# Moving a token-block border of an interleaved second GEMM next to an AV run, and one filler step with it

## The chip, the cores and the metric

The kernel runs on one core of a Trainium2 chip. The metric is the device time of a run in microseconds (us), the median over the runs of one kernel. The span of a profiled execution goes from the first to the last instruction and is some 2 us shorter than the run's time. All runs used here were classed as being in the fast state. Some of them show a granted TensorE clock of 0.988 to 0.995 instead of 1.0 and are 1 to 3 us longer; where such runs matter, this is said. Others are as much longer at a clock of 0.999 to 1.0 (350.76 us for the kernel before, 347.15 for one of the variants); why is not known. Small differences between median times are therefore not relied on alone here, but with the distances within a stage, which repeat almost exactly.

## The reference

Attention with a decay ("forgetting") term for 8 batches of 8 heads, 576 tokens and head size 64, then a two-layer network with the exact GELU on the 4608 token rows:

```python
scores = scale * q @ k.T ; decay = cum[:, :, :, None] - cum[:, :, None, :]     # cum = cumsum(log(clip(f)))
attn   = softmax(where(causal, scores + decay, -1e9))
x      = (attn @ v)  -> rows of 512
h      = x @ w_in                  # 512 -> 2048
out    = gelu(h) @ w_out           # 2048 -> 512
```

## The kernel before

Batches come one after another. An attention stage works through four pairs of heads, and each pair has four score tiles (0 to 3): matmuls into a PSUM tile with two buffers, an exp on ScalarE that reads it, and a mask on GpSimd (POOL). ScalarE can't keep up with bare score matmuls (an exp of a 128x896 tile takes 0.92 us, the matmuls of that tile 0.36), so TensorE does the **second GEMM of the previous batch** between the score tiles. This filler comes in steps from a generator. After tile 1 of each pair come the 30 matmuls of attention times V (the "AV run") of the pair before.

```python
PLAN = [                                   # token block, who lends the two banks, the 16 steps
    (0, "o", 16 * "r"),
    (1, "m", 6 * "r" + "n" + 9 * "r"),
    (2, "m", "n" + 9 * "r" + "n" + 5 * "r"),
    (3, "s", 7 * "r" + 9 * "n"),
]

def gemm2_rows(c, plan):
    for ts, held, steps in plan:
        ...                                # banks[0], banks[1]: two PSUM tiles of the pool "held"
        for kt, step in enumerate(steps):
            last = kt == steps.rindex("r")
            for r in range(2 if step == "r" else 1):
                rows = slice(r * D, (r + 1) * D) if step == "r" else slice(0, P)
                nc.tensor.matmul(banks[r], g_of[c][kt][rows, ...], w_out_sb[rows, kt, :], ...)   # L466
            if kt == n_ff - 1 if held == "s" else last:
                nc.vector.tensor_copy(ot, banks[1])                                              # L474
            if kt == n_ff - 1:
                nc.vector.tensor_tensor(ot, ot, banks[0], Alu.add)                               # L476
                store(c, ts, ot)
            yield

FILL = [[7, 6, 3, 3], [1, 3, 3, 3], [1, 3, 3, 3], [1, 3, 3, 3], [7]]     # steps after tile t of pair i

def attention(b):                          # b = 2 takes other counts and another plan
    ...
    for i in range(HP):
        for t in range(4):
            scores(b, i, t)                # score matmuls L289, exp L299, mask L301
            take(fill, counts[i][t])
            if i and t == 1:
                av(i - 1)                  # AV run L320, then normalize on DVE (L333, L334)
            ...
    take(fill, counts[HP][0])
    av(HP - 1)
    take(fill, 6)
    ...
    take(fill, 999)
```

An "r" step is two matmuls of 64 rows into two banks, which use the two halves of the array side by side (both matmuls of the r step at 198.88 us lie within 0.38 us, and one alone takes 0.38), as the score matmuls do (two at 198.68 within 0.36). An "n" step is one matmul of all 128 rows into banks[0], as the AV matmuls are. At the end of a block DVE copies banks[1] out and adds banks[0] to it. Blocks 1 and 2 both take the two banks of pool "m", which has just two. The bank that the copy frees is the one that block 2 gets as banks[0]: in the trace the n step that opens block 2 starts at 202.27 us, right after the copy (201.52 to 202.21) and during the add (202.25 to 202.94). After the attention stage comes the first GEMM of the batch (L375), with GELU on ScalarE.

The softmax here doesn't subtract the row's maximum and nothing guards it: scores larger than these inputs give would overflow.

Of the kernel before, what the change touches and what calls it, by code (L numbers as in the profile page):

```python
# [52 lines left out]
def kernel(  # L53
# [340 lines left out]
    def gemm2(c):  # L394
# [35 lines left out]

    PLAN = [
        (0, "o", 16 * "r"),
        (1, "m", 6 * "r" + "n" + 9 * "r"),
        (2, "m", "n" + 9 * "r" + "n" + 5 * "r"),
        (3, "s", 7 * "r" + 9 * "n"),
    ]

# [8 lines left out]
    def gemm2_rows(c, plan):  # L446




        for ts, held, steps in plan:
            if held == "s":
                both = s_psum.tile([P, 2, d_model], FP32, tag="s", name="ps2")
                banks = [both[:, 0], both[:, 1]]
            else:
                pool = {"o": o_psum, "m": m_psum}[held]
                banks = [
                    pool.tile([P, d_model], FP32, tag=held, name="ps2")
                    for _ in range(2)
                ]  # L460
            ot = o_pool.tile([P, d_model], FP32, tag="ot", name="ot")
# [4 lines that stand above are left out]
                    nc.tensor.matmul(  # L466
                        banks[r],
                        g_of[c][kt][rows, ts * P : (ts + 1) * P],
                        w_out_sb[rows, kt, :],
                        start=kt == (steps.index("r") if r else 0),  # L470
                        stop=last if r else kt == n_ff - 1,
# [7 lines that stand above are left out]
# [37 lines left out]
    def gemm2_third():  # L516
        yield from gemm2_half(0, 1)
        yield from gemm2_rows(0, PLAN_0)
        yield from gemm2_rows(1, PLAN_1)
# [94 lines left out]



    FILL = [[7, 6, 3, 3], [1, 3, 3, 3], [1, 3, 3, 3], [1, 3, 3, 3], [7]]
    FILL_2 = [[8, 8, 8, 8], [8, 8, 4, 4], [4, 4, 4, 4], [4, 4, 4, 4], [8]]
    FILL_1 = [[0, 0, 0, 0], [0, 0, 0, 0], [2, 2, 2, 2], [2, 2, 2, 2]]

    def attention(b):


        fill = gemm2_third() if b == 2 else gemm2_rows(b - 1, PLAN)
        counts = FILL_2 if b == 2 else FILL

# [135 lines left out]
```

## Time and profile before

| | before |
|---|---|
| time, median of 3 runs (range) | 348.35 us (348.30 to 348.62) |
| span of the profiled run | 345.7 us |
| TensorE busy | 328.3 us, 95% |
| TensorE's idle time ahead of the filler, waiting for the DVE copy L474 | 3.9 us in 5 waits |
| from the start of AV run 0 in one stage to that in the next | 36.16 us |

In a line of the grouped view the figures after the first bar are the busy time in us and the mean ns of one instruction; after the second bar stands the idle time of the engine just before these instructions, and what ended most of it. In a timeline line they are the start, the duration, the engine, the line of the program, the operation and its count; what stands in brackets is the idle time before it and its releaser. Lines that follow each other on one engine are merged, so a count of six is three r steps.

### The profile page before, as it was taken

Reading aid. Unit: us, or ns where it says so; the run is one execution under the profiler, and the core shown is the slowest. Engines: PE = TensorE matmul, PEld = TensorE weight load, DVE = VectorE, ACT = ScalarE, POOL = GpSimd, SP = SyncE. Lnnn points to the kernel's source line nnn. Section 1 sums busy time; section 2 is a strip of 40 time slices with the busy share of each in tenths; the row PEclk is TensorE's granted clock in tenths of the full one; section 3 lists DMA queues with packets and bytes.
Section 4 is the critical chain, followed back from the end, with each engine's and each line's share of the span. In section 5 each row is a group of like instructions: output and inputs, shape, how many; then the busy total and the mean of one; then the engine's idle time right before and its main releaser. Section 6 shows DMA issues by size and latency. Waiting matters only on the chain.

```text
span 345.7 us, 7895 instructions
## 1 busy us (share of the span) xinstructions
PE 328.3 (95%) x3187; PEld 173.7 (50%) x3227; DVE 188.1 (54%) x424; ACT 212.1 (61%) x296; POOL 125.1 (36%) x256
## 2 busy tenths in 40 slices
PE   7899999999999999999899989998999899999995
PEld 3674555445554455545554555445544554444443
DVE  5670456934367935795479647974597542020011
ACT  5976786773634787368746874687468765503600
POOL 8390673128418044533345333624261430000000
PEclk9999999999999999999999999999999999999999
DMA  8999999979992999488935995498900230011013
GB/s 116 176 171 194 202 178 147 170 149 161 222 183 100 138 202 176 81 119 167 219 89 81 134 211 137 74 161 190 170 30 2 69 83 30 2 61 61 0 35 89
DMA packets 99924, 43.03 MB, mean 124 GB/s; under 512 B 78704, under 2 KB 95344, under 8 KB 99888
## 3 DMA queue, kind: packets, MB, share of 16 engines
q1 hardware_dynamic: 82592, 28.37, 42.4%
q0 software_dynamic: 16896, 13.63, 26.9%
q8 instruction: 25, 0.41, 0.5%
q10 hardware_dynamic: 400, 0.52, 0.4%
q14 instruction: 11, 0.09, 0.1%
HBM read 36.85 MB, written 9.44 MB: 134 GB/s over the span
## 4 chain that ended last, share of the span: by engine, by line
PE 89%; DVE 4%; ACT 3%; issue 2%; POOL 2%; POOLq 0%; ACTq 0%; DVEq 0%
PE ps L375 35%; PE ps L466 25%; PE o L320 9%; PE ps L408 8%; PE s L289 8%; ACT e L299 2%; PE ps L501 2%; PE ps_x L353 1%; DVE ot L474 1%; PE ps_f L206 1%; DVE x L334 1%; POOL q L107 1%; POOL k L107 1%; DVE qT L213 0%; DVE kT L213 0%
## 5 line engine op out<-in xcount | busy, mean ns | idle before, releaser
L392 ACT ACTIVATE g<-ps 128x512 bf16<-128x512 f32 x144 | 85.3, 597 | 80.2 <-PE ps L375 80.2
L299 ACT ACTIVATE e<-s 128x896 bf16<-128x896 f32 (+2 forms) x128 | 101.0, 836 | 32.1 <-PE s L289 28.2
L375 PE MATMUL ps<-xT,w_in_sb 128*128 128x512 bf16 x497 | 111.4, 379 | 0.8
L466 PE MATMUL ps<-w_out_sb,g 64*128 64x512 bf16 (+1 forms) x736 | 104.0, 376 | 4.7 <-DVE ot L474 3.9
L375 PEld LDWEIGHTS <-w_in_sb 128*128 128x128 bf16 x576 | 56.0, 98 | 67.5 <-issue 1.8
L301 POOL TENSOR_SCALAR_AFFINE_SELECT e<-e 128x256 bf16<-128x256 bf16 (+1 forms) x135 | 49.5, 385 | 100.1 <-ACT e L299 99.9
L466 PEld LDWEIGHTS <-g 64*128 64x128 bf16 (+1 forms) x756 | 39.8, 94 | 40.4 <-issue 10.6
L244 DVE COPY qT<-tq 64x288 bf16<-64x288 bf16 x96 | 49.3, 514 | 1.4
L260 POOL TENSOR_TENSOR vw<-v_sb,wT 128x640 bf16<-128x640 f32 x31 | 39.6, 1279 | 24.7 <-DMA v_sb<-in_v_dram 24.5
L289 PE MATMUL s<-qT,kT 64*128 64x320 bf16 (+4 forms) x384 | 43.9, 277 | 3.3 <-ACT e L299 2.6
L320 PE MATMUL o<-vw,e 128*128 128x65 bf16 x960 | 36.8, 194 | 2.7 <-issue 2.4
L320 PEld LDWEIGHTS <-e 128*128 128x128 bf16 x960 | 34.8, 98 | 9.2 <-POOL e L301 4.1
L474 DVE COPY ot<-ps 128x512 f32<-128x512 f32 x26 | 17.9, 690 | 35.5 <-PE ps L466 35.5
L244 DVE COPY kT<-tk 64x288 bf16<-64x288 bf16 x96 | 33.0, 344 | 1.6
L334 DVE TENSOR_TENSOR x<-o,r 128x320 bf16<-128x320 f32 x64 | 31.5, 492 | 2.2
L417 DVE COPY ot<-ps 128x512 f32<-128x512 f32 (+2 forms) x9 | 5.7, 632 | 48.8 <-PE ps L408 31.9
L289 PEld LDWEIGHTS <-kT 64*128 64x128 bf16 x384 | 18.7, 94 | 22.6 <-issue 7.3
L333 DVE RECIPROCAL r<-o 128x5 f32<-128x5 f32 x64 | 12.2, 190 | 30.8 <-PE o L320 30.7
L408 PE MATMUL ps<-w_out_sb,g 128*128 128x512 bf16 (+2 forms) x142 | 27.9, 355 | 0.1
L408 PEld LDWEIGHTS <-g 128*128 128x128 bf16 x144 | 13.5, 98 | 14.5
L476 DVE TENSOR_TENSOR ot<-ot,ps 128x512 f32<-128x512 f32 x26 | 17.9, 687 | 1.2
L375 PE MATMUL ps<-tails,w_in_sb 128*128 128x512 bf16 x63 | 14.3, 377 | 0.1
(64 smaller groups left out, 148.2 us busy)
## 6 DMA issues: line engine op xcount, KB each, us to landing
out_dram<-ot SPq DMA_DIRECT2D x32, 256.0 KB, 2.3
v_sb<-in_v_dram SPq DMA_DIRECT2D x24, 256.0 KB, 5.7
q<-in_q_dram POOLq DMA_DIRECT2D x6, 576.0 KB, 6.2
k<-in_k_dram POOLq DMA_DIRECT2D x6, 576.0 KB, 8.2
v_sb<-in_v_dram SPq DMA_DIRECT2D x22, 128.0 KB, 5.3
w_in_sb<-in_moe_w_in_dram POOLq DMA_DIRECT2D x4, 512.0 KB, 7.0
w_out_sb<-in_moe_w_out_dram POOLq DMA_DIRECT2D x4, 512.0 KB, 8.4
q<-in_q_dram POOLq DMA_DIRECT2D x4, 144.0 KB, 4.5
```

What stands on the lines that cost most here:

```text
L244: nc.vector.tensor_copy(rows[:, odd], src[odd * D : (odd + 1) * D, 2 * i + h].rearrange("d j p -> d p j"),)
L260: eng.tensor_tensor(vw_of[b][:, hs, :, 0:D], v_sb[:, hs, :, :], w.unsqueeze(3).to_broadcast([P, 2, NBLK, D]), Alu.mult,)
L289: nc.tensor.matmul(to, *ab, start=half < 0, stop=half == 1 or not masked)
L299: nc.scalar.activation(et[:, :, z:c], st[:, :, z:c], Act.Exp, scale=scale)
L301: nc.gpsimd.affine_select(out=et[:, :, c0 + z : c0 + P], in_=et[:, :, c0 + z : c0 + P], compare_op=Alu.is_ge, fill=0.0, base=z, pattern=[[ ...
L320: nc.tensor.matmul(o[:, m, :], e_of[b, i, t][:, h, c : c + P], vw_of[b][:, 2 * i + h, n, :], start=(n == 0), stop=(n == m),)
L334: nc.vector.tensor_tensor(x_of[b, i][:, :, h, :], o[:, :, 0:D], r.unsqueeze(2).to_broadcast([P, NBLK, D]), Alu.mult,)
L375: nc.tensor.matmul(ps, w_in_sb[:, kt, ffb * P : (ffb + 1) * P], src[:, kt, 0:TC], start=(kt == 0), stop=(kt == n_dm - 1),)
L392: nc.scalar.activation(g_of[c][ffb], ps, Act.Gelu)
L408: nc.tensor.matmul(pss[ts][:, c0:c1], g_of[c][kt][:, ts * P : (ts + 1) * P], w_out_sb[:, kt, c0:c1], start=(kt == 0), stop=(kt == n_ff - 1),)
L466: nc.tensor.matmul(banks[r], g_of[c][kt][rows, ts * P : (ts + 1) * P], w_out_sb[rows, kt, :], start=kt == (steps.index("r") if r else 0), ...
L474: nc.vector.tensor_copy(ot, banks[1])
```

## The change

The border between blocks 1 and 2 moves from one step ahead of AV run 1 to AV run 1 itself, so that the eviction of block 1 can lie beside the AV matmuls. For this the fill gives up one step after tile 3 of pair 1 and takes it back ahead of AV run 3; the n steps are placed again so that each AV run follows one.

```diff
-        (1, "m", 6 * "r" + "n" + 9 * "r"),
-        (2, "m", "n" + 9 * "r" + "n" + 5 * "r"),
+        (1, "m", 6 * "r" + "n" + 8 * "r" + "n"),
+        (2, "m", 9 * "r" + "n" + 6 * "r"),
...
-    FILL = [[7, 6, 3, 3], [1, 3, 3, 3], [1, 3, 3, 3], [1, 3, 3, 3], [7]]
+    FILL = [[7, 6, 3, 3], [1, 3, 3, 2], [1, 3, 3, 3], [1, 3, 3, 3], [8]]
```

The five stages of batches 3 to 7 use these tables.

## The prediction

> **Names.** An attention stage (batches 3 to 7, so five of them) runs four head pairs, 0 to 3, and for each pair four score tiles, 0 to 3. Between score tiles it puts filler: 64 steps of the previous batch's second GEMM, 16 for each of four token blocks. An r step is two 64-row matmuls into two PSUM banks, an n step is one 128-row matmul into one bank. AV p is the run of 30 AV matmuls of pair p, issued after tile 1 of pair p+1. Steps are numbered 0 to 63.
>
> **What bounds the kernel now.** I read the page first: engine shares, then the chain of waits.
>
> ```profile
> PE 328.3 (95%) x3187; PEld 173.7 (50%) x3227; DVE 188.1 (54%) x424; ACT 212.1 (61%) x296; POOL 125.1 (36%) x256
> PE 89%; DVE 4%; ACT 3%; issue 2%; POOL 2%; POOLq 0%; ACTq 0%; DVEq 0%
> L466 PE MATMUL ps<-w_out_sb,g 64*128 64x512 bf16 (+1 forms) x736 | 104.0, 376 | 4.7 <-DVE ot L474 3.9
> ```
>
> TensorE is the bound: 95% busy and 89% of the chain. The granted clock digit is 9 in all 40 slices, so the clock is not in question. The third line is the filler; TensorE stood idle 4.7 us before it, 3.9 of them for the DVE copy that empties a PSUM bank. The view of that copy line and the list of waits of TensorE both give this as 3.9 us in 5 waits, longest 0.8: one for each of the five stages. From 123 us on, where the five stages lie, the list has nothing else but 2.4 us of "issue" ahead of AV runs; the other waits lie in the first two batches, which the change doesn't touch. The timeline of TensorE in one stage (batch 4) shows where the wait is:
>
> ```profile
> 196.71 0.33 PE L289 MATMUL s<-qT,kT 64*128 64x64 bf16 x4
> 196.88 0.60 PE L466 MATMUL ps<-w_out_sb,g 64*128 64x512 bf16 x4
> 197.63 1.12 PE L320 MATMUL o<-vw,e 128*128 128x65 bf16 x30 [0.16 <-issue]
> ...
> 200.72 0.33 PE L289 MATMUL s<-qT,kT 64*128 64x64 bf16 x4
> 200.88 0.60 PE L466 MATMUL ps<-w_out_sb,g 64*128 64x512 bf16 x4
> 202.27 0.38 PE L466 MATMUL ps<-w_out_sb,g 128*128 128x512 bf16 x1 [0.79 <-DVE ot L474]
> 202.48 1.11 PE L320 MATMUL o<-vw,e 128*128 128x65 bf16 x30
> ```
>
> Both groups are the same work: tile 1, two r steps, an n step, an AV run. (In the first the record of the n matmul is missing, although its weight load is in the trace; hence the "issue" gap.) From tile 1 to AV 0 it takes 197.63 - 196.71 = 0.92 us, and AV 2 gives 0.92 too; to AV 1 it takes 202.48 - 200.72 = 1.76. The difference, 0.84 us, is the cost of the wait. Its reason is in the plan: step 31, an r step, ends block 1, and step 32, the n step, opens block 2 in the same two "m" banks with nothing between them.
>
> [...] the trace has 692 for the copy, 687 for the add, so the two take about 1.4 us one after the other. [...] for the two shapes of exp that matter below; the trace has 917 and 698. [...] on the chain nine r steps of batch 4 fill 0.65 us per three, 0.217 each. I use 0.21 to 0.22 us a step, r or n.
>
> **The change part by part.** It adds and removes no instruction: on every engine the program order has as many rows as before, only places differ; SyncE's order is the same.
>
> (1) Fill: tile 3 of pair 1 is followed by two steps instead of three, and the run before AV 3 gets eight instead of seven. So AV 0 still comes after step 22, AV 1 after step 31 (was 32), AV 2 after 41 (was 42), AV 3 after 55 (same).
>
> (2) Plan: block 1 ends in an n step (31), block 2 begins with an r step (32) and has its n at 41. The number of n steps and of changes between r and n is the same; each AV run still has one n step ahead of it. The border of blocks 1 and 2 now has AV 1 and tile 2 of pair 2 between its sides. The 0.79 us wait ahead of AV 1 must go: that n step now writes into its own block's open bank. **Removed: 0.84 us a stage.**
>
> (3) Does the eviction hide? Put in the clock of the stage above, before this change: the copy starts after the last r step, at 201.52, and ends at 202.21; the add runs 202.25 to 202.94. AV 1 would start at 200.72 + 0.92 = 201.64, tile 2 of pair 2 at 201.64 + 1.05 = 202.69 and step 32 some 0.20 later, at 202.89. Its first matmul goes to the bank that the copy freed long ago, the second to the one that the add frees at 202.94; with the 0.06 us that the wait in the trace took from the copy's end to the matmul (202.21 to 202.27) that is 203.00. **Left over: about 0.1 us.**
>
> (4) One step fewer between tile 3 of pair 1 and tile 0 of pair 2 brings tiles 0 and 1 of pair 2 forward by 0.21 us. There are two score buffers, so tile 1 of pair 2 needs the exp of tile 3 of pair 1 to be done. ScalarE in a stretch of that stage:
>
> ```profile
> 199.15 1.51 ACT L299 ACTIVATE e<-s 128x896 bf16<-128x896 f32 x2 [0.74 <-PE s L289]
> 199.96 0.70 ACT L299 ACTIVATE e<-s 128x640 bf16<-128x640 f32 x1
> ```
>
> The two lines are from two narrow windows; the first merges the exps of tiles 2 and 3, the second is tile 3 alone. It ends at 199.96 + 0.70 = 200.66; tile 1 started at 200.72, without a wait, only just. Tile 0 is all right: its buffer is free at 199.15 + 0.92 = 200.07, plus 0.06, and it would come at 200.10. Tile 1 would come at 200.72 - 0.21 = 200.51 and must wait until about 200.72. **New: 0.21 us**, exactly the step taken out: it becomes idle time there and is paid later, ahead of AV 3.
>
> The sum for a stage: -0.84 + 0.21 + 0.10 = -0.53 us. Five stages: -2.65 us. TensorE is on the path through the rest of the stage and the first GEMM after it, so what it gains is gained at the end: 348.35 - 2.65 = **345.7 us**, 0.8% less.
>
> **Rivals.** (A) No new wait: the removed time is all kept, 5 x 0.84 = 4.2 us, 344.15 us. For it: my figures in (3) and (4) are differences of 0.1 to 0.2 us, near the trace's grain, and the second r matmul may hide a late bank. Against: 200.72 against 200.66 is read directly, and a buffer can't be written before its exp. (B) The wait moves: the two DVE operations still take 1.4 us, and the normalize of AV 1 now queues behind both (it ends at 204.4 in the clock above, some 2.8 us after AV 1 began instead of 2.0). If the next AV run or the transpose DMA of this pair had waited for it, the gain would be gone, 348 us. Against: AV 2 comes 4.0 us after AV 1, and the transposed tile is first read at the GEMM at 213.8. (C) Another engine becomes the bound, or DMA does: ScalarE is 61% busy, and had 0.74 us idle just before the two lines above; DVE is 54%, DMA is near 9 tenths in many slices but no TensorE wait for a DMA is in the list of waits. A stage of 36.2 us that shrinks by 0.5 leaves this as it is. It would give 347 to 348.5. (D) Slower by more than the noise would need a fresh wait over 0.84 us per stage; I see none.
>
> **Range and chances.** The ground is regular: the five waits are 0.78 or 0.79 us and the three runs lie within 0.32 us. Between A (344.15) and a half-lost gain (347.2) lies most of what I can imagine; 8 in 10 for 344.5 to 347.0. Over 2% faster would be below 341.4, more than all the waits that the change can reach; over 2% slower would be 355.3. I give each 1%.
>
> **What would show it right or wrong.** In the changed trace: the wait of the filler for the copy of line 474 (3.9 us) is gone; tile 1 of pair 2 to AV 1 takes 0.92 instead of 1.76 us in each stage; a wait of tile 1 of pair 2 for an exp, some 0.2 us five times, in the list of waits; at step 32 a wait for the add of line 476 of 0.1 us or less; the stage's period falls from 36.2 to about 35.6 us; the first GEMM's stretches keep their 14 us. The prediction is wrong if tile 1 shows no such wait (then 344 to 345), if step 32 waits by several tenths, or if something later (the transposes before the first GEMM, untangling) takes back what was gained.

## The result and the profile after

| | before | changed |
|---|---|---|
| median (range), 4 runs each | 348.33 us (347.60 to 348.62) | 345.50 us (345.24 to 346.67) |
| ratio, 95% interval | 1 | 0.9928 (0.9900 to 0.9956) |
| span of the profiled run | 345.7 us | 343.4 us |

A ratio is the mean time of one kernel's fast runs over the mean of the other's fast runs of the same rounds, so it isn't quite the ratio of the medians. The change saves 0.7%, within the 2% that counts as the same.

The page of the changed kernel, engine shares and the line of the filler:

```profile
PE 328.6 (96%) x3182; PEld 174.7 (51%) x3227; DVE 187.0 (54%) x424; ACT 212.3 (62%) x296; POOL 124.2 (36%) x256
L466 PE MATMUL ps<-w_out_sb,g 64*128 64x512 bf16 (+1 forms) x731 | 103.0, 376 | 0.8 <-issue 0.8
```

The work is the same and the span is 2.3 us shorter. The 3.9 us of waits for the copy are gone.

The timeline of TensorE in the changed kernel, in the stage that the prediction showed of before, from tile 3 of pair 1 on:

```profile
198.77 0.30 PE L289 MATMUL s<-qT,kT 64*128 64x320 bf16 x2
198.91 0.59 PE L466 MATMUL ps<-w_out_sb,g 64*128 64x512 bf16 x4
199.36 0.37 PE L289 MATMUL s<-qT,kT 64*128 64x256 bf16 x4
199.55 0.39 PE L466 MATMUL ps<-w_out_sb,g 64*128 64x512 bf16 x2
199.95 0.34 PE L289 MATMUL s<-qT,kT 64*128 64x64 bf16 x4
200.12 0.61 PE L466 MATMUL ps<-w_out_sb,g 64*128 64x512 bf16 x4
200.88 1.11 PE L320 MATMUL o<-vw,e 128*128 128x65 bf16 x30 [0.16 <-issue]
201.93 0.36 PE L289 MATMUL s<-qT,kT 64*128 64x448 bf16 x2
202.13 0.97 PE L466 MATMUL ps<-w_out_sb,g 64*128 64x512 bf16 x6
202.78 0.30 PE L289 MATMUL s<-qT,kT 64*128 64x320 bf16 x1
202.91 0.38 PE L466 MATMUL ps<-w_out_sb,g 64*128 64x512 bf16 x1
202.94 0.29 PE L289 MATMUL s<-qT,kT 64*128 64x320 bf16 x1
```

Three things are to be seen. Tile 1 of pair 2 (199.95) to AV 1 (200.88) takes 0.93 us; before it took 1.76. Tile 0 to tile 1 of that pair takes 199.95 - 199.36 = 0.59 us; one r step lies between them, which makes 0.40 to 0.41 in pair 1 (195.55 to 195.96). And after AV 1 the two halves of the array fall out of step: the two matmuls of a score tile, together at 198.77 (both within 0.30 us, the time of one), start at 202.78 and 202.94.

DVE around the border, first before, then changed:

```profile
201.52 0.69 DVE L474 COPY ot<-ps 128x512 f32<-128x512 f32 x1 [1.86 <-PE ps L466]
202.25 0.69 DVE L476 TENSOR_TENSOR ot<-ot,ps 128x512 f32<-128x512 f32 x1
```

```profile
200.76 0.69 DVE L474 COPY ot<-ps 128x512 f32<-128x512 f32 x1 [1.86 <-PE ps L466]
201.56 0.69 DVE L476 TENSOR_TENSOR ot<-ot,ps 128x512 f32<-128x512 f32 x1
```

The eviction now runs from 200.76 to 202.25, beside AV 1 (200.88 on). It takes 1.49 us instead of 1.42: the add begins 0.11 us after the end of the copy (200.76 + 0.69 = 201.45) instead of 0.04.

ScalarE in the changed kernel, from two narrow windows, for the gap ahead of tile 1: the exps of tiles 2 and 3 of pair 1, and those of tile 3 and the next one:

```profile
198.39 1.51 ACT L299 ACTIVATE e<-s 128x896 bf16<-128x896 f32 x2 [0.74 <-PE s L289]
...
199.20 1.56 ACT L299 ACTIVATE e<-s 128x640 bf16<-128x640 f32 x2
```

The exp of tile 3 ends at 198.39 + 1.51 = 199.90 and tile 1 of pair 2, which takes over its buffer, starts at 199.95. In the same way the exp of tile 2 ends at 199.31 (198.39 + 0.92) and tile 0 of pair 2 starts at 199.36.

For the whole stage I measure from AV run to AV run and, at the spot above, from tile 0 to tile 1 of pair 2. The stages of one kernel agree to 0.02 us, with one exception that is named below. "Stage" is from AV 0 to the AV 0 of the next stage; columns are us.

| kernel | AV 0 to AV 1 | AV 1 to AV 2 | AV 2 to AV 3 | tile 0 to 1, pair 2 | stage |
|---|---|---|---|---|---|
| before | 4.85 | 4.00 | 4.33 | 0.41 | 36.16 |
| changed | 4.00 | 4.17 | 4.51 | 0.59 | 35.67 |

AV 0 to AV 1 has a step fewer in the changed kernel, AV 2 to AV 3 a step more. A stage gains 0.49 us, five gain 2.45. The span lost 2.3, because AV 0 of the first of these stages came 0.23 us later in the changed profile (125.53 against 125.30), where the two programs are still the same.

### The profile page after: what moved, and what is told of

Same layout as the page of the kernel before. It is cut to its first block, busy times and chain, and to the rows that moved or that the text cites. A ratio compares the mean times of both kernels' runs of the same rounds, so it can differ in the third digit from the quotient of the medians.

```text
span 343.4 us, 7895 instructions
## 1 busy us (share of the span) xinstructions
PE 328.6 (96%) x3182; PEld 174.7 (51%) x3227; DVE 187.0 (54%) x424; ACT 212.3 (62%) x296; POOL 124.2 (36%) x256
## 4 chain that ended last, share of the span: by engine, by line
PE 89%; issue 2%; POOL 2%; DVE 2%; ACT 2%; DMA 2%; POOLq 0%; ACTq 0%; DVEq 0%
PE ps L375 36%; PE ps L466 25%; PE o L320 9%; PE ps L408 8%; PE s L289 7%; PE ps L501 2%; ACT e L299 2%; DMA k<-in_k_dram 2%; PE ps_x L353 1%; DVE x L334 1%; POOL q L107 1%; PE ps_f L206 1%; POOL k L107 1%; DVE r L333 0%; DVE xT L356 0%
## 5 line engine op out<-in xcount | busy, mean ns | idle before, releaser
L466 PEld LDWEIGHTS <-g 64*128 64x128 bf16 (+1 forms) x756 | 41.5, 94 | 40.4 <-issue 11.9
L289 PE MATMUL s<-qT,kT 64*128 64x320 bf16 (+4 forms) x384 | 45.8, 276 | 3.6 <-ACT e L299 2.7
L474 DVE COPY ot<-ps 128x512 f32<-128x512 f32 x26 | 17.9, 689 | 37.1 <-PE ps L466 35.2
L289 PEld LDWEIGHTS <-kT 64*128 64x128 bf16 x384 | 19.5, 94 | 23.2 <-issue 9.7
L476 DVE TENSOR_TENSOR ot<-ot,ps 128x512 f32<-128x512 f32 x26 | 17.9, 687 | 1.5
L365 POOL COPY tails<-xT 128x256 bf16<-128x256 bf16 x8 | 3.2, 399 | 31.3 <-DVE xT L356 31.3
```

The source lines that it names most:

```text
L289: nc.tensor.matmul(to, *ab, start=half < 0, stop=half == 1 or not masked)
L466: nc.tensor.matmul(banks[r], g_of[c][kt][rows, ts * P : (ts + 1) * P], w_out_sb[rows, kt, :], start=kt == (steps.index("r") if r else 0), ...
```

## The experiments

My theory: the kernel before lost 0.84 us a stage since PSUM banks were taken again before DVE had emptied them; the changed kernel hides the eviction beside the AV run, but pays two new, smaller waits, one for an exp and one for the add. The rivals: that the order of n and r steps is what helps; that a border has to lie at an AV run, so nothing else would do; and that the two small gaps have other causes. The 95% intervals of the ratios of the changed kernel and of the versions with one remedy overlap (0.9900 to 0.9956 against 0.9879 to 0.9919 and 0.9882 to 0.9932), so what decides between them is the stage's distances in the traces. The first four kernels ran together on one chip (before: 348.23 us), the next three on another occasion (before: 348.20), the last three on a third (before: 348.11). All gave correct results.

### The plan alone

```diff
 PLAN as in the change; FILL as before
```

> The new plan (block 1 ends with an n step, block 2 opens with r) with the old fill counts, so AV 1 still comes after step 32, which is now an r step that opens block 2 ahead of AV 1. My theory (the eviction must lie beside the AV run): the opening r step now needs both banks, so it waits for copy and add, and AV 1 starts about 0.6 us later than before; two more changes between r and n add up to 0.1 us each. +0.6 to +0.9 us in each of five stages: 351.3 to 352.8 us. The rival (the plan itself, with its better order of n steps, is what helps, and the fill counts are cosmetic) expects 345 to 346 us.

Measured: 352.90 us (352.27 to 355.17), ratio 1.0141 (1.0114 to 1.0168). TensorE around the border:

```profile
167.28 0.70 PE L466 MATMUL ps<-w_out_sb,g 64*128 64x512 bf16 x3
168.45 0.37 PE L466 MATMUL ps<-w_out_sb,g 64*128 64x512 bf16 x1 [0.46 <-DVE ot L474]
169.24 0.37 PE L466 MATMUL ps<-w_out_sb,g 64*128 64x512 bf16 x1 [0.42 <-DVE ot L476]
169.54 0.42 PE L320 MATMUL o<-vw,e 128*128 128x65 bf16 x8
```

The opening r step waits twice: its first matmul for the copy, its second for the add. AV 0 to AV 1 takes 5.51 us, 0.66 more than before, and the stage 37.06, 0.90 more; 5 x 0.90 = 4.5 us, beside 4.7 in the time, just above the range expected. Of the 0.90 us, 0.22 lie between AV 1 and AV 2 (4.22 instead of 4.00), where nothing waits: n step 41 is followed by an r step ahead of AV 2, and such a lone n step has a cost that the next experiment shows. So the plan by itself is harmful: it opens the block with a step that needs both banks, and parts an n step from its AV run. Of the kernels run here, it is good only with the fill counts that bring the border to an AV run.

### The fill counts alone

```diff
 PLAN as before; FILL as in the change
```

> The old plan with the new fill counts: AV 1 comes after step 31, so the border of the blocks is at AV 1, but the n steps 32 and 42 now come after an AV run and a score tile, among r steps, and the AV runs 1 and 2 follow an r step. My theory (what counts is that the AV run lies between the last step of block 1 and the first of block 2): most of the gain stays, since the n step that opens block 2 needs only the bank freed first and then finds it free; the cost is two n steps among r steps, an estimated 0.1 to 0.2 us each a stage. About 346 to 347 us. The rival (the n step next to the AV run is the point) expects 348 us or more. Waits of 0.79 us for the copy: none.

Measured: 346.79 us (346.49 to 347.17), ratio 0.9957 (0.9942 to 0.9973). No wait for the copy or the add is in the list. Stage: 35.93 us, with 3.99 us from AV 0 to AV 1, 4.22 from AV 1 to AV 2 and 4.73 from AV 2 to AV 3. The border's place thus brings about half of the changed kernel's gain by itself (0.23 of 0.49 us a stage). What is missing against the changed kernel are its two n steps among r steps, shown by the time from tile 2 to tile 3 of pairs 2 and 3, 1.06 us each with the n step first in between (timeline of TensorE, the score matmuls alone):

```profile
166.70 0.36 PE L289 MATMUL s<-qT,kT 64*128 64x448 bf16 x2
...
167.76 0.30 PE L289 MATMUL s<-qT,kT 64*128 64x320 bf16 x2
...
170.92 0.36 PE L289 MATMUL s<-qT,kT 64*128 64x448 bf16 x2
...
171.98 0.30 PE L289 MATMUL s<-qT,kT 64*128 64x320 bf16 x2
```

With three r steps in between it is 0.84 or 0.85. A single full-array step among half-array work costs 0.21 us more than an r step. An n step among its like is no slower than an r step: six in a row take 1.30 us in the kernel before (211.76 to 213.06), 0.217 each, so I put the 0.21 us down to the two changes between whole-array and half-array work, some 0.1 us each. What in a change takes this time, no run separates. (The "up to 0.1 us each" of the plan alone and the "0.1 to 0.2 us" here were my estimates before these runs.) The sum closes: against the changed kernel 2 x 0.21 more, 0.16 less for the second small wait, which is absent here, makes +0.26 us, and the stage is 0.26 longer.

### The step taken out elsewhere

```diff
-    FILL = [[7, 6, 3, 3], [1, 3, 3, 2], ...        # changed
+    FILL = [[7, 6, 3, 3], [1, 2, 3, 3], ...
-        (1, "m", 6 * "r" + "n" + 8 * "r" + "n"),
+        (1, "m", 5 * "r" + "n" + 9 * "r" + "n"),
```

> The changed kernel, but the step is taken out after tile 1 of pair 1 (ahead of AV 0) instead of after tile 3 of pair 1; its n step moves to 21, so AV 0 still follows an n step, and the border stays at AV 1. My theory says that the changed kernel pays about 0.2 us a stage because tile 1 of pair 2 waits for the exp of tile 3 of pair 1; here the spacing of these tiles is the old one and that wait should go: tile 0 to tile 1 of pair 2 takes 0.41 us again instead of 0.59, 5 x 0.18 = 0.9 us less than the changed kernel, about 344.6 us. The rival (that gap is no wait for the exp but a delay in TensorE's own order, or the wait only moves to another tile) expects 345.5 us.

Measured: 344.59 us (344.19 to 346.11), ratio 0.9899 (0.9879 to 0.9919); again, on the third occasion, 344.84 us (344.05 to 347.21), ratio 0.9911 (0.9878 to 0.9943), beside 345.73 for the changed kernel.

> Only the step taken out ahead of AV 0, in the same rounds as the version with both: 344.6 us as before, some 0.8 us more than with both.

Tile 0 to tile 1 of pair 2 takes 0.40 us again and the stage 35.45 us, 0.22 less than in the changed kernel; 5 x 0.22 = 1.1 us. AV 0 comes one step earlier and no wait appears in its place, as ScalarE had 0.74 us idle there in the changed kernel and still has 0.53 here. The gap of 0.59 us was therefore the wait for the exp: same steps, same border, only the spacing of the tiles restored. Of the repeated runs two, at 346.7 and 347.2 us, have granted clocks of 0.995 and 0.990; the other four lie at 344.05 to 345.01. The first of the two is the profiled one. Its clock was low only ahead of the five stages (0.96 in the first 40 us, 1.00 from then on), and its stages take 35.45 us too, but for one of 35.97: there the first GEMM waited 0.35 us for the DMA that transposes x. No other profile shows this wait in the five stages.

### Two n steps at the end of block 1

```diff
-        (1, "m", 6 * "r" + "n" + 8 * "r" + "n"),       # changed
+        (1, "m", 6 * "r" + "n" + 7 * "r" + 2 * "n"),
```

> The changed kernel, but block 1 ends with two n steps instead of one (6 r, n, 7 r, 2 n), so that the copy of the second bank can start one step earlier and the add right after it. My theory: the changed kernel pays 0.16 us a stage after AV 1 since the second matmul of step 32 waits for the add; here the add ends some 0.2 us earlier and the delay goes: AV 1 to AV 2 takes 4.00 us as in the kernel before instead of 4.17, 5 x 0.16 = 0.8 us less than the changed kernel, about 344.7 us. The rival (the delay there has another cause, such as the score tiles) expects 345.5 us.

Measured: 344.59 us (344.44 to 347.15), ratio 0.9907 (0.9882 to 0.9932). TensorE, then DVE:

```profile
200.62 1.11 PE L320 MATMUL o<-vw,e 128*128 128x65 bf16 x30
201.66 0.36 PE L289 MATMUL s<-qT,kT 64*128 64x448 bf16 x2
201.86 0.81 PE L466 MATMUL ps<-w_out_sb,g 64*128 64x512 bf16 x6
202.51 0.30 PE L289 MATMUL s<-qT,kT 64*128 64x320 bf16 x2
```

```profile
200.28 0.69 DVE L474 COPY ot<-ps 128x512 f32<-128x512 f32 x1 [1.65 <-PE ps L466]
201.07 0.69 DVE L476 TENSOR_TENSOR ot<-ot,ps 128x512 f32<-128x512 f32 x1
```

The add ends at 201.76, ahead of the opening r step at 201.86; in the changed kernel it ended at 202.25, behind that step's start at 202.13. The three r steps are back to 0.81 us from 0.97, the score matmuls start as a pair, and AV 1 to AV 2 takes 4.00 us instead of 4.17. The second small wait was the one for the add. (The changed kernel was not in these rounds; its figures come from its own traces, in which AV 1 to AV 2 takes 4.16 or 4.17 us in every stage.)

### Both remedies

```diff
 FILL as with the step taken out elsewhere
+        (1, "m", 5 * "r" + "n" + 8 * "r" + 2 * "n"),
         (2, "m", 9 * "r" + "n" + 6 * "r"),
```

> Both remedies in one: the step is taken out ahead of AV 0, and block 1 ends with two n steps. If the two small losses of the changed kernel (0.18 us at tile 1 of pair 2, 0.16 us after AV 1) are what I take them for and independent, both go: 5 x 0.34 = 1.7 us less than the changed kernel, about 343.8 us. If ScalarE or the POOL masking bounds the stage at that pace, the sum will not be reached: 344.5 or more.

Measured: 344.66 us (343.62 to 347.57), ratio 0.9901 (0.9860 to 0.9942). The six runs scatter, and the profiled one of them had a granted clock of 0.988; the run doesn't decide whether the two gains add. It was repeated, with the changed kernel and the first remedy in the same rounds:

> The version with both remedies once more, since its first runs scattered (343.6 to 347.6 us) and its profiled run had a granted clock of 0.988. In the first trace its stage took 35.29 us against 36.16 before: 348.3 - 5 x 0.87 = 343.9 us. If the remedies were not additive in time, it would be no better than 344.6 us, the time of each remedy alone.

> The changed kernel in the same rounds as the two others, for a comparison on one chip: 345.6 us, 0.9 us over the step ahead of AV 0 and 1.7 us over both remedies.

Measured: 343.82 us (343.64 to 344.14, 5 runs), ratio 0.9870 (0.9843 to 0.9897); the changed kernel 345.73 us, ratio 0.9923. The difference is 1.9 us, against 1.7 expected from 5 x 0.34. The stage takes 35.29 us, in both profiles of this kernel: in the first, the low clock (0.91) lies in the first 40 us, and AV 0 of the first of the five stages comes 3.2 us later than in the second (128.70 against 125.46). Against the changed kernel that is 35.67 - 35.29 = 0.38 us a stage, so the two gains add. Of the 0.87 us gained on before, 0.84 is the old wait, which is now gone with nothing in its place:

```profile
198.72 0.36 PE L289 MATMUL s<-qT,kT 64*128 64x256 bf16 x4
198.91 0.38 PE L466 MATMUL ps<-w_out_sb,g 64*128 64x512 bf16 x2
199.13 0.33 PE L289 MATMUL s<-qT,kT 64*128 64x64 bf16 x4
199.29 0.38 PE L466 MATMUL ps<-w_out_sb,g 64*128 64x512 bf16 x2
199.83 0.38 PE L466 MATMUL ps<-w_out_sb,g 128*128 128x512 bf16 x1 [0.16 <-issue]
200.05 1.11 PE L320 MATMUL o<-vw,e 128*128 128x65 bf16 x30
```

(The 0.16 us of "issue" stands for a missing record of the first of two n steps.) Here tile 1 comes 0.41 us after tile 0 and AV 1 0.92 us after tile 1.

### The border left where it was, an earlier copy

```diff
 FILL as before
-        (1, "m", 6 * "r" + "n" + 9 * "r"),             # before
+        (1, "m", 6 * "r" + "n" + 6 * "r" + 3 * "n"),
```

> The kernel before with its old fill counts and its border ahead of AV 1, but block 1 ends with three n steps, so that its second bank is copied out three steps ahead of the border. The n step that opens block 2 then finds the bank free, and no border has to move. My theory (the cost was the 0.79 us from the last r step to the end of the copy, and nothing else about the border): the wait goes, 5 x 0.84 = 4.2 us less, less an n step among r steps (0.1 to 0.2 us a stage): 344.2 to 345.2 us. The rival (the border has to lie at an AV run) expects little: 347 to 348 us.

Measured: 345.13 us (344.73 to 345.74), ratio 0.9899 (0.9870 to 0.9927). A border need not lie at an AV run. With the last r step three steps ahead of the end, the copy runs from 163.86 to 164.55, while block 1 goes on in its other bank, and the first step of block 2 finds an empty one; the list of TensorE's waits in the five stages is empty. The loss is an n step among score tiles (the three n steps are the last before the border, and the first of them stands alone between tiles 0 and 1 of pair 2; timeline of all engines, TensorE's matmuls and DVE's copy alone):

```profile
163.66 0.35 PE L289 MATMUL s<-qT,kT 64*128 64x256 bf16 x4
...
163.86 0.69 DVE L474 COPY ot<-ps 128x512 f32<-128x512 f32 x1 [0.86 <-PE ps L466]
...
163.94 0.39 PE L466 MATMUL ps<-w_out_sb,g 128*128 128x512 bf16 x1
...
164.27 0.34 PE L289 MATMUL s<-qT,kT 64*128 64x64 bf16 x4
```

Tile 0 to tile 1 is 0.61 us here, 0.20 more than with an r step, and the stage takes 35.53 us: 0.63 less than before, as 0.84 - 0.20 gives.

### The changed kernel again

> The changed kernel once more, with the two others on one chip, so that they can be compared within the same rounds: 345.5 us.

Measured: 346.01 us (344.90 to 347.11), ratio 0.9931 (0.9898 to 0.9963). The three ratios of the changed kernel are 0.9928, 0.9931 and 0.9923. This trace also settles a point of reading: it has the records of all 756 filler matmuls, and with them the 0.16 us of "issue" ahead of the AV runs is gone, from 2.4 us to none in the list. Those gaps were missing records, not idle time. The same holds for an entry that could be taken for the new wait: the first trace of the changed kernel lists 0.8 us in 5 waits of AV runs for the add, but they are ahead of AV 3 (209.56, 0.16 us), where the n step's record is missing, and are gone from the full trace.

All kernels side by side, with the stage's distances (us):

| kernel | AV 0 to AV 1 | AV 1 to AV 2 | AV 2 to AV 3 | tile 0 to 1, pair 2 | stage |
|---|---|---|---|---|---|
| plan alone | 5.51 | 4.22 | 4.34 | 0.41 | 37.06 |
| fill alone | 3.99 | 4.22 | 4.73 | 0.59 | 35.93 |
| step out ahead of AV 0 | 4.01 | 4.16 | 4.51 | 0.40 | 35.45 |
| two n steps | 4.01 | 4.00 | 4.51 | 0.60 | 35.51 |
| both remedies | 4.00 | 4.01 | 4.51 | 0.41 | 35.29 |
| earlier copy, old border | 4.21 | 4.01 | 4.32 | 0.61 | 35.53 |

## Why the prediction was right

The time (345.7 predicted, 345.5 measured) and its class came out as predicted, and so did the mechanism; one term of the sum was too small. That the medians agree to 0.2 us is partly luck: 2.65 us less was predicted, and the three occasions gave 2.83, 2.19 and 2.38; the stages give 2.45. The parts:

- **The old wait.** 0.84 us a stage was to go; tile 1 to AV 1 went from 1.76 to 0.93 us. That it was the eviction and not the place or the order as such is shown by the earlier copy at the old border, which removes the wait too, and by the plan alone, which makes it longer.
- **The new wait for the exp.** 0.21 us predicted; of it 0.18 shows between tiles 0 and 1 (0.59 against 0.41), and taking the step out elsewhere shows the cause. The whole step is lost: AV 0 to AV 1 takes 4.00 us with a step fewer, and 4.85 - 0.84 = 4.01 is what it would take with that step. The small rest lies at tile 0, which the prediction called all right although its own figures had the buffer free at 200.13 and the tile at 200.10; it started 0.05 us after the exp of tile 2. So rival A, no new wait, is out.
- **The rest of the eviction.** "About 0.1 us" was too small: AV 1 to AV 2 grew by 0.17. The working had the add begin 0.04 us after the copy, as before; it begins 0.11 after. In the kernel before one r step ended both banks, and in the changed one the last matmul of the second bank is another instruction than that of the first. The same 0.10 to 0.11 is seen with the plan alone and with two n steps, where the order is the same, and 0.03 to 0.04 with the fill counts alone, where it is the old one. The traces show one thing more: in the changed kernel, which has the delay, the adds (L476) have nine semaphore instructions on DVE's queue, each of 21 ns, in the kernel before four, so one more for each of the five stages. I take the delay for the handling of a second, separate wait on TensorE; no run isolates this. With it the term would have been 0.17.
- **The sum.** -0.53 us predicted for a stage, -0.49 measured. With 0.17 for the eviction the prediction's own sum would be -0.46; the step added ahead of AV 3 took 0.18 us (4.51 against 4.33) instead of 0.21, which makes up the rest. Why it took less is not shown.
- **Rivals B and C.** Nothing later took the gain back: the normalize of AV 1, which did move behind the eviction, held nobody up. As for another bound, the best version still gets the stage down by 0.87 us, and has an empty list of TensorE waits for the five stages in the first of its two profiles.

Two things were wrong though they did not move the number. The list of waits does not show the new wait for the exp, as the prediction said it would: the modelled ends of the matmuls before it (0.39 us for an r step that takes 0.21) cover it, and only the distances between starts show it. The wait for the add at step 32 is hidden in the same way. And the stage that the prediction calls batch 4 is that of batch 5; the stages are alike, so nothing hangs on it.

## What to carry to other kernels

Where two accumulation groups follow each other in the same PSUM banks, look at what TensorE does between the last matmul of the one and the first of the other; work that uses other banks belongs there, or the group can be made to finish one of its banks early (here either took away the loss of 0.84 us a stage). Each filler step moved also changes the spacing of the tiles around it, so check for each buffer whether its reader will be done by the new time, to a tenth of a microsecond: here the step taken out in one place was lost to a wait (0.59 us from tile 0 to tile 1 of pair 2), and in another it cost nothing (0.40). Measure such small waits by the distance between starts of like instructions, not by the idle time that the profile lists.

## Small times measured here

- One 128-row matmul of 512 columns among pairs of 64-row matmuls cost 0.20 to 0.21 us more than a pair of 64-row ones (0.61 against 0.41 us with the earlier copy at the old border, 1.06 against 0.85 with the fill counts alone).
- In the kernel before, the PSUM-to-SBUF copy of 128x512 fp32 took 692 ns (median of L474), and the fp32 add of the same shape with one operand in PSUM 687 (L476).
- A waiting matmul started 0.06 us after the end of a DVE copy (202.21 to 202.27, kernel before) and 0.05 after that of an exp (199.90 to 199.95, changed kernel).
- In the changed kernel the two 64-row halves stay out of step for a while: the second matmul of step 32 starts at 202.29, 0.16 us after the first (202.13), and in the two score tiles after it that half is still 0.16 us behind (202.78 and 202.94, 203.56 and 203.72); a filler matmul starts in between (202.91).
